# A third raw query block in the last two heads, with part of its subtractions on VectorE, and three late gate and up tiles moved into the rounds

## The chip, the cores and the metric

The kernel runs on one core of one Trainium2 chip. A core has a matrix engine (TensorE, PE in the profile), VectorE (DVE), ScalarE (ACT), GpSimd (POOL) and SyncE (SP), which here only issues transfers. Each engine works through its own instructions in order, and they wait for each other by semaphores. Matrix results go to PSUM, everything else lies in SBUF. The metric is the time of one execution in microseconds of device time; less is better.

## The reference

The result is a mix of an attention block and a gated MLP, with a gate per row:

```python
x = A_x                                             # 1 x 2048 x 448
g = _sigmoid((x * gate_w).sum(-1, keepdims=True))
# attention, 16 heads of 28 columns
scores = jnp.einsum("bhqd,bhkd->bhqk", q, k) * (Dh ** -0.5)
p = _softmax(scores, axis=-1)
a = einsum("bhqk,bhkd->bhqd", p, v) ... @ wo
# MLP, 1792 hidden columns
gate = gate * (gate > 0)
b = (gate * up) @ W_down
return g * a + (1 - g) * b
```

All is float32. The kernel splits most matmul operands into a high and a low part and sums several products (`TERMS`, 11 products for one contraction).

## The kernel before

**Stages.** First come the projections to Q, K and V. Then come 32 *rounds*, two for each of the 16 heads: round v works on *visit* v, which is head v // 2 with one half of its 2048 keys. Last comes a tail with the down projection of the MLP, the output projection and the result.

**A visit.** The 2048 queries of a head are four blocks j = 0 to 3 of 512 queries; the visit's 1024 keys are eight chunks of 128. A *score pair* (`score`, letter s) is two matmuls of 128 keys x 512 queries into one PSUM tile of two banks. There are three such tiles in turn (`ps_w`). A visit has 16 pairs, four for each block. Four chunks of one block are a *quad* in SBUF, 128 x 2048; ten slots hold quads.

**Two ways to the softmax.** The scores need a maximum per query subtracted before the exponential.

- A block that is not raw gets its maximum beforehand: TensorE computes scores the other way round (`smax`, letter m, two matmuls into a PSUM tile) and VectorE reduces them (L228, 128 x 1024). The maxima are written as two extra rows into Q, and the score matmul subtracts them by itself. ScalarE then takes the exponential straight from PSUM (L334).
- A *raw* block needs no maxima from TensorE. ScalarE copies its negated scores to SBUF (L336). VectorE takes a running minimum over the pairs (`block_min`, letter b, L280; three instructions for four pairs, and all but the first pair are read from PSUM, so the tile is held until then). `all_max` (letter A, L295 to L303) reduces over the partitions and spreads the result over a tile `rm`. GpSimd subtracts `rm` from each of the block's two quads (`take_max`, letter g, L309, 128 x 2048), and ScalarE takes the exponential in SBUF (L320; letter e half a quad, E a whole one). When the second visit of a head changes the maximum, the first visit's sums are rescaled (`rescale`, letters c and f).

`RAW` names the raw blocks of each visit: blocks 3 and 2 everywhere, except in the very first visit. So the maxima of a head are 16 pairs: two blocks x four groups of 128 queries x two halves.

**P and Q** (`pv`) multiply the exponentials with V, 64 TensorE instructions for the two parts of a round. P needs the first quad of every block, Q the second.

**x** is one matmul of the projections that are computed between the attention's: until round 3 part of Q and K (L641), then gate and up of the MLP (L633). 22 x's are one tile of 128 hidden columns x 512 rows: 11 for gate, then 11 for up. Its result h is stored to memory (`spill_h`). There are 56 tiles; `done` of them are computed in the rounds, the rest (`gate_up`) in the tail.

**The order** is written out by hand, one letter for each step: `ROUNDS` holds a string for each round. Each letter issues its instructions to all the engines that take part, and every engine keeps the order in which they were issued; nothing reorders them. Four score pairs of the next visit are always issued in the round ahead (`AHEAD`). Other letters: n ends a head's maxima, N normalises the head before, w splits a weight tile, D prepares the first weights of the down projection.

**The tail.** A list `todo` is worked off: 12 matmuls for each of 56 hidden tiles (`down`), whose operand h is fetched and split by ScalarE and VectorE (L136, L142), the remaining `gate_up` tiles between, and the output projection (`wout`) when the last head has been normalised, stored, fetched again and split.

Of the kernel before, what the change touches and what calls it, by code (L numbers as in the profile page):

```python
# [8 lines left out]
F32 = mybir.dt.float32  # L9
# [3 lines left out]
OP = mybir.AluOpType  # L13
AX = mybir.AxisListType
# [4 lines left out]
P = 128  # L19
# [7 lines left out]
NF = F // P  # L27
NB = 4
# [9 lines left out]

RAW = [(3,), (3, 2), (3, 2), (3, 2)]

# [6 lines left out]
NP = 10  # L47

R11 = "ssbnsxxxxsxbxNxbxxggsxxxxsxxxsxsxxssxxAmxsxxemsxmxexxmxsmxxemmgexsbxxxsbcxxxsbxAxmgeePefeQ"

R12 = "gsmsxxxxssebxxbbxxxsxxxxmxAexxssxgsxxsxxsxxmxxsxxemsmexgxexmxxxmsxmxexsbxsgebsebAPQ"

# [21 lines left out]

R29 = "sxxsxsxxxbxgxsxxbsxExsxxxxxxxxxbxssxsxAxxxsxgNxxsxsxxxssxxxxgxsxxxExxxbxgxxbxExsexxcxexfxPbAQn"

R30 = "sgsxxsbxxsxxxxxbxxgxEbxxxxxsxxxxxsssxxxxxsxxsxAsxxxxexgxxxxsxsExxxsexxxbgxxxxsexbxxsexDDbxPQA"

R31 = "sxsxxsxxxbxxxxxsbbxxxxxxxgsxxxxsxxssxxxxAsxxsxxgxgxgExxxDxxxxNxxxExxEsexcexxsxxfxxxDxPQ"

# [3 lines left out]
    R12, R11, R12, R11, R12, R11, R12, R11,  # L84
    R12, R11, R12, R11, R12, R29, R30, R31,
]
# [13 lines left out]
def gated_mix_kernel(ctx, tc, x, wq, wo, wgu, wd, out):  # L100
# [101 lines left out]
    def raw(v):  # L202

        return RAW[v] if v < len(RAW) else RAW[len(RAW) - 2 + v % 2]

# [85 lines left out]
    def all_max():  # L291
        v, j, quads = todo_all.pop(0)
        to = ((0, 11) if j == 2 else (9, 10))[v % 2]
        a, b = (1 - v % 2, 9) if j == 2 else (1, 9 + v % 2)
        nc.vector.tensor_reduce(MN[:, 1:3], R2.pop((v, j)).rearrange("p a (b r) -> p a b r", r=32), axis=AX.X, op=OP.min,  # L295
                                apply_transpose=True)
        move(MN[:64, 3:5], MN[64:, 1:3])
        move(MN[:32, 5:9], MN[32:64, 1:5])
# [4 lines left out]
        nc.vector.transpose(RM[v, j], MN[:, to].unsqueeze(2).to_broadcast([P, 16, 32]))  # L303
        todo_sub.extend((v, j, q) for q in quads)

    def take_max():
        v, j, q = todo_sub.pop(0)
        m = RM[v, j].unsqueeze(1).to_broadcast([P, 4, TB])
        nc.gpsimd.tensor_tensor(QUAD[q], QUAD[q], m, op=OP.subtract)  # L309
        todo_exp.append(q)  # L310
# [355 lines left out]
    def rescale(v, part):  # L666

        h = v // 2
        if v % 2 == 0:
            return  # L670
        rows = slice(64, P)
        if part == 0:
            RS[h] = fe.tile([P, TB], F32, name=f"rs_{h}", tag="rb", bufs=1)
            for r, a, b in ((slice(64, 96), 11, 0), (slice(96, P), 10, 9)):
                nc.gpsimd.tensor_tensor(MN[r, 1], MN[r, a], MN[r, b], op=OP.subtract)
            nc.vector.transpose(RS[h][rows], MN[rows, 1].unsqueeze(2).to_broadcast([64, 16, 32]))
        else:
# [97 lines left out]
    for v, order in enumerate(ROUNDS):  # L775
# [4 lines left out]
        for o in order:  # L780
# [159 lines left out]
    def down(i):  # L940
# [6 lines left out]
        if f == NF - 1:  # L947
# [9 lines left out]
            (fetch_w, 6), (fetch_w, 7), (lambda: wor.append(load_wo()),), (fetch_h, 6), (gate_up, done), (spread, H - 1),  # L957
            (split_wd, 4), (fetch_w, 8), (split_wd, 5), (fetch_w, 9), (fetch_h, 7), (gate_up, done + 1)]
    for i in range(NB * NF):
# [63 lines left out]
```

## Time and profile before

| | us |
|---|---|
| median of 3 runs | 1185.54 (1185.16 to 1185.97) |
| the profiled execution | 1184.21 |
| its span from the first to the last instruction | 1182.4 |
| TensorE matmuls busy | 1175.0 |
| VectorE busy | 894.1 |
| ScalarE busy | 877.2 |
| GpSimd busy | 743.3 |
| rounds 25 to 31 (794.1 to 985.8) | 191.7 |
| the tail (985.8 to 1182.4) | 196.6 |

A row of the profile names the line, the engine, the operation, the tiles as out<-in, the shapes and the count; behind the bar stand the busy time, the mean duration of one in ns, and the idle time of the engine ahead of these instructions with what ended it. In a timeline row the start and the duration stand first. PEld is TensorE's loading of weights, which runs beside its matmuls. Matmul durations in the rows overlap, so the cost of one is read from the distance of many.

### The profile page before, as it was taken

Reading aid. Unit: us, or ns where it says so; the run is one execution under the profiler, and the core shown is the slowest. Engines: PE = TensorE matmul, PEld = TensorE weight load, DVE = VectorE, ACT = ScalarE, POOL = GpSimd, SP = SyncE. Lnnn points to the kernel's source line nnn. Section 1 sums busy time; section 2 is a strip of 40 time slices with the busy share of each in tenths; the row PEclk is TensorE's granted clock in tenths of the full one; section 3 lists DMA queues with packets and bytes.
Section 4 is the critical chain, followed back from the end, with each engine's and each line's share of the span. In section 5 each row is a group of like instructions: output and inputs, shape, how many; then the busy total and the mean of one; then the engine's idle time right before and its main releaser. Section 6 shows DMA issues by size and latency. Waiting matters only on the chain.

```text
span 1182.4 us, 17006 instructions
## 1 busy us (share of the span) xinstructions
PE 1175.0 (99%) x6183; PEld 821.2 (69%) x6183; DVE 894.1 (76%) x1173; ACT 877.2 (74%) x1054; POOL 743.3 (63%) x325
## 2 busy tenths in 40 slices
PE   9999999999999999999999999999999999999998
PEld 6886666666666666666666666666666667899997
DVE  6577898888988898989898888889898553444242
ACT  5237889899999988888888887888888885322121
POOL 5323667888988886777777766767676784422020
PEclk9999999999999999999999999999999999999999
DMA  9994565636373754343446535153444437644342
GB/s 322 280 394 142 186 210 172 185 124 196 117 216 108 205 167 139 119 128 92 119 136 212 140 102 153 49 152 109 139 154 156 129 100 231 209 152 118 115 134 75
DMA packets 70667, 188.85 MB, mean 160 GB/s; under 512 B 13958, under 2 KB 20558, under 8 KB 65678
## 3 DMA queue, kind: packets, MB, share of 16 engines
q1 hardware_dynamic: 65624, 167.31, 45.9%
q0 software_dynamic: 4480, 19.99, 4.5%
q8 instruction: 48, 0.79, 0.3%
q10 hardware_dynamic: 480, 0.47, 0.1%
q14 instruction: 35, 0.29, 0.1%
HBM read 126.96 MB, written 60.96 MB: 159 GB/s over the span
## 4 chain that ended last, share of the span: by engine, by line
PE 96%; DVE 1%; DMA 1%; ACT 1%; issue 0%; SPq 0%; DVEq 0%; ACTq 0%
PE gu L633 24%; PE s L330 20%; PE po L692 19%; PE acc L927 12%; PE sm L224 10%; PE v L469 3%; PE wo L886 3%; PE qk L641 3%; PE qk L454 2%; DVE r L280 1%; DMA wr<-wq 0%; DMA X<-x_d 0%; ACT P L336 0%; ACT V L336 0%; SPq L414 0%
## 5 line engine op out<-in xcount | busy, mean ns | idle before, releaser
L309 POOL TENSOR_TENSOR P<-P,rm 128x2048 f32<-128x2048 f32 x102 | 470.8, 4635 | 107.9 <-DVE rm L303 84.1
L633 PE MATMUL gu<-X,wg 128*128 128x512 f32 x1232 | 358.9, 395 | 0.1
L228 DVE TENSOR_REDUCE mx<-sm 128x1 f32<-128x1024 f32 x256 | 302.9, 1217 | 43.0 <-PE sm L224 42.1
L330 PE MATMUL s<-Q,K 128*128 128x512 f32 x1024 | 315.9, 403 | 1.7 <-DVE mx L228 0.9
L633 PEld LDWEIGHTS gu<-X,wg 128*128 128x128 f32 x1232 | 231.2, 188 | 57.6 <-issue 1.7
L330 PEld LDWEIGHTS s<-Q,K 128*128 128x128 f32 x1024 | 180.7, 188 | 82.4 <-DVE r L280 10.4
L336 ACT ACTIVATE P<-s 128x1024 f32<-128x1024 f32 x204 | 202.2, 1028 | 42.0 <-PE s L330 39.6
L692 PE MATMUL po<-P,V 128*32 128x512 f32 x1640 | 227.4, 594 | 0.0
L334 ACT ACTIVATE P<-s 128x1024 f32<-128x1024 f32 x206 | 201.4, 1040 | 14.1 <-PE s L330 13.1
L320 ACT ACTIVATE P<-P 128x1024 f32<-128x1024 f32 (+1 forms) x182 | 208.5, 1171 | 0.5 <-POOL P L309 0.2
L224 PE MATMUL sm<-K,Q 128*128 128x512 f32 x520 | 163.2, 400 | 0.1
L280 DVE SCALAR_TENSOR_TENSOR r<-s,r 128x1024 f32<-128x1024 f32 x124 | 151.6, 1223 | 13.6 <-ACT P L336 6.0
L692 PEld LDWEIGHTS po<-P,V 128*32 128x32 f32 x1640 | 62.6, 110 | 113.3 <-issue 109.6
L692 PE MATMUL po<-V 128*32 128x512 f32 x408 | 136.2, 594 | 0.0
L309 POOL TENSOR_TENSOR V<-V,rm 128x2048 f32<-128x2048 f32 x24 | 111.2, 4635 | 26.1 <-DVE rm L303 22.6
L224 PEld LDWEIGHTS sm<-K,Q 128*128 128x128 f32 x520 | 91.9, 188 | 34.1 <-ACT P L334 4.6
L136 ACT ACTIVATE hh<-hr 128x512 fp32r<-128x512 f32 x52 | 32.8, 632 | 109.5 <-PE acc L927 109.4
L142 DVE TENSOR_TENSOR hh<-hr,hh 128x512 fp32r<-128x512 f32 x52 | 47.3, 915 | 72.6 <-ACT hh L136 72.5
L927 PE MATMUL acc<-WD,hh 128*128 128x448 f32 x480 | 99.5, 366 | 0.0
L927 PEld LDWEIGHTS acc<-WD,hh 128*128 128x128 f32 x480 | 90.2, 188 | 7.3 <-DVE hh L142 0.2
L280 DVE SCALAR_TENSOR_TENSOR r<-s,P 128x1024 f32<-128x1024 f32 x50 | 61.1, 1223 | 33.3 <-ACT P L336 33.0
L295 DVE TRANSPOSE_TENSOR_REDUCE mn<-r 128x32 f32<-128x1024 f32 x63 | 78.1, 1239 | 1.3
(93 smaller groups left out, 1135.5 us busy)
## 6 DMA issues: line engine op xcount, KB each, us to landing
wg<-ws_d SPq DMA_DIRECT2D x42, 896.0 KB
K<-qk_d SPq DMA_DIRECT2D x32, 448.0 KB
X<-x_d SPq DMA_DIRECT2D x56, 256.0 KB
h_d<-h SPq DMA_DIRECT2D x56, 256.0 KB
Q<-qk_d SPq DMA_DIRECT2D x62, 224.0 KB
hr<-h_d SPq DMA_DIRECT2D x52, 256.0 KB
ws_d<-wg SPq DMA_DIRECT2D x14, 896.0 KB
x_d<-X POOLq DMA_DIRECT2D x8, 1024.0 KB, 15.2
```

The lines of the kernel that those rows point to most:

```text
L224: nc.tensor.matmul(ps[:, c, :], Q[h][:, u * P:(u + 1) * P], K[h % 3][:, k0:k0 + TB], start=True, stop=True)
L228: nc.vector.tensor_reduce(to, ps, axis=AX.XY, op=OP.max)
L280: nc.vector.scalar_tensor_tensor(r, ps, -1.0, before, op0=OP.mult, op1=OP.min)
L295: nc.vector.tensor_reduce(MN[:, 1:3], R2.pop((v, j)).rearrange("p a (b r) -> p a b r", r=32), axis=AX.X, op=OP.min, apply_transpose=True)
L309: nc.gpsimd.tensor_tensor(QUAD[q], QUAD[q], m, op=OP.subtract)
L320: nc.scalar.activation(q, q, AF.Exp, scale=-SCALE)
L330: nc.tensor.matmul(ps[:, c], K[h % 3][:, k * P:(k + 1) * P], Q[h][:, j * TB:(j + 1) * TB], start=True, stop=True)
L334: nc.scalar.activation(dst, ps, AF.Exp, scale=SCALE)
L336: nc.scalar.activation(dst, ps, AF.Copy, scale=-1.0)
L633: nc.tensor.matmul(ps, WS[i][:, s, a], xf(i // NF, b), start=(n == 0), stop=(n == NT - 1))
L692: nc.tensor.matmul(po[32 * j:32 * j + 32], V[:, h // 4 % 2, k, h % 4], AT.pop((v, k, j)), start=(k == k0), stop=(k == k0 + NK // 2 - 1))
L927: nc.tensor.matmul(ACC[i // NF][t][:, :D], HH[i][:, a, t * P:(t + 1) * P], wd_high_low(f, b), start=(f == 0 and n == 0), stop=(f == NF - 1 ...
```

## The change

- In visits 28 to 31, the last two heads, block 1 is raw too (`RAW`). Their maxima are then for block 0 alone, 8 pairs a head instead of 16. The third raw block gets its own columns of the small tile `MN` in `all_max`, and `rescale` covers all four blocks' rows there.
- A new letter G is a subtraction of `rm` that is issued to VectorE instead of GpSimd: one in round 25, two in 26, one in 28, two in 29, one in 30, two in 31.
- Three more gate and up tiles, 66 x's, are in the rounds (`done` is 55 instead of 52), so the tail has one left.
- The strings of rounds 25 to 31 are new. Rounds 0 to 24 are as before; their strings only stand in another order in the file.

```diff
-RAW = [(3,), (3, 2), (3, 2), (3, 2)]
+RAW = [(3,)] + [(3, 2)] * 27 + [(3, 2, 1)] * 4
...
-R30 = "sgsxxsbxxsxxxxxbxxgxEbxxxxxsxxxxxsssxxxxxsxxsxAsxxxxexgxxxxsxsExxxsexxxbgxxxxsexbxxsexDDbxPQA"
+R28 = "sxxssbbgsbxxxExxsgxxxxsxsxxxsAxEbxxgxxxxxbxxxbxxgAxsxsxxxxxxGsxssxxxxxmxxmExsEgxxxxbxxxxxxExsxesbbexAPQxxx"
...
+R30 = "DxxDxsxsxxxxxgbxsxgbssxxbxsExxxAxsxxxxbsbxxbxxExxxgxxxAxxxxgsxGsxxsxxsxsExExsxxExxgexessxxxxxxbxbxxxxxxxPQxxbA"
...
-    R12, R11, R12, R11, R12, R29, R30, R31,
+    R12, R25, R26, R27, R28, R29, R30, R31,
...
-        to = ((0, 11) if j == 2 else (9, 10))[v % 2]
-        a, b = (1 - v % 2, 9) if j == 2 else (1, 9 + v % 2)
+        c = 12 if j == 1 else 0
+        to = ((12, 21), (0, 11), (9, 10))[j - 1][v % 2]
+        a, b = (c + 1 - v % 2, c + 9) if j < 3 else (1, 9 + v % 2)
...
-    def take_max():
+    def take_max(engine):
         v, j, q = todo_sub.pop(0)
         m = RM[v, j].unsqueeze(1).to_broadcast([P, 4, TB])
-        nc.gpsimd.tensor_tensor(QUAD[q], QUAD[q], m, op=OP.subtract)
+        engine.tensor_tensor(QUAD[q], QUAD[q], m, op=OP.subtract)
         todo_exp.append(q)
...
-    MN = att.tile([P, 12, 16], F32, name="mn")
+    MN = att.tile([P, 22, 16], F32, name="mn")
...
-        rows = slice(64, P)
+        more = 1 in raw(v)
+        rows = slice(0 if more else 64, P)
...
-            for r, a, b in ((slice(64, 96), 11, 0), (slice(96, P), 10, 9)):
+            for r, a, b in ((slice(0, 32), 21, 21), (slice(32, 64), 21, 12), (slice(64, 96), 11, 0), (slice(96, P), 10, 9))[0 if more else 2:]:
...
-            elif o == "g":
-                take_max()
+            elif o in "gG":
+                take_max(nc.gpsimd if o == "g" else nc.vector)
```

In the rows of the order below, `r2_28_1` is the running minimum of visit 28, block 1; `rm_28_1` the spread maximum; `P_28_1_0` (or `V_103`, two slots that lie in V) a quad of this block; `sm` a tile of the maxima's scores; `h_44` the product of a gate and up tile. Line numbers of the change are 8 to 10 higher.

VectorE in round 28, behind the spreading of block 2's maximum. Before:

```order
L303 STREAM_TRANSPOSE rm_28_2_8082<-mn_891 128x512
L707 RECIPROCAL rq_13_8090<-ls_13_8017 128x16
L228 TENSOR_REDUCE mx_15_7864<-sm_254_8128 128x1
L652 TENSOR_TENSOR h_43_8142<-gu_43_1_8088,rl_43_8086 128x512
L228 TENSOR_REDUCE mx_15_7864<-sm_255_8149 128x1
```

Now:

```order
L312 STREAM_TRANSPOSE rm_28_2_8058<-mn_891 128x512
L288 SCALAR_TENSOR_TENSOR r2_28_1_8062<-s_28_2_1_8032,P_28_1_0_8014 128x1024
L288 SCALAR_TENSOR_TENSOR r2_28_1_8062<-s_28_4_1_8038,r2_28_1_8062 128x1024
L661 TENSOR_TENSOR h_43_8076<-gu_43_1_8045,rl_43_8043 128x512
L288 SCALAR_TENSOR_TENSOR r2_28_1_8062<-s_28_6_1_8048,r2_28_1_8062 128x1024
L304 TENSOR_REDUCE mn_891<-r2_28_1_8062 128x32
...
L312 STREAM_TRANSPOSE rm_28_1_8093<-mn_891 128x512
L318 TENSOR_TENSOR P_28_1_0_8014<-P_28_1_0_8014,rm_28_1_8093 128x2048
L236 TENSOR_REDUCE mx_15_7811<-sm_242_8135 128x1
L236 TENSOR_REDUCE mx_15_7811<-sm_243_8141 128x1
```

A second block's minima and reduction and one subtraction (L318) now stand where there were only maxima, and the two maxima that are left stand behind the subtraction.

GpSimd in the same round. Before:

```order
L309 TENSOR_TENSOR P_28_3_0_7910<-P_28_3_0_7910,rm_28_3_7969 128x2048
L309 TENSOR_TENSOR V_103<-V_103,rm_28_3_7969 128x2048
L309 TENSOR_TENSOR V_103<-V_103,rm_28_2_8082 128x2048
L309 TENSOR_TENSOR P_28_2_1_8042<-P_28_2_1_8042,rm_28_2_8082 128x2048
```

Now:

```order
L318 TENSOR_TENSOR P_28_3_0_7867<-P_28_3_0_7867,rm_28_3_7938 128x2048
L318 TENSOR_TENSOR V_103<-V_103,rm_28_3_7938 128x2048
L318 TENSOR_TENSOR V_103<-V_103,rm_28_2_8058 128x2048
L318 TENSOR_TENSOR P_28_2_1_7993<-P_28_2_1_7993,rm_28_2_8058 128x2048
L318 TENSOR_TENSOR P_28_1_1_8037<-P_28_1_1_8037,rm_28_1_8093 128x2048
```

GpSimd has a fifth subtraction, for the second quad of block 1; the first quad's is VectorE's.

VectorE in round 29, behind the last spreading of a maximum of this visit (block 2 before, block 1 now). Before:

```order
L303 STREAM_TRANSPOSE rm_29_2_8353<-mn_891 128x512
L652 TENSOR_TENSOR h_45_8385<-gu_45_1_8339,rl_45_8328 128x512
L280 SCALAR_TENSOR_TENSOR r2_30_3_8421<-s_30_2_3_8396,P_30_3_0_8391 128x1024
L280 SCALAR_TENSOR_TENSOR r2_30_3_8421<-s_30_4_3_8407,r2_30_3_8421 128x1024
L676 STREAM_TRANSPOSE rs_14_8438<-mn_891 64x512
```

Now:

```order
L312 STREAM_TRANSPOSE rm_29_1_8395<-mn_891 128x512
L318 TENSOR_TENSOR V_103<-V_103,rm_29_1_8395 128x2048
L686 STREAM_TRANSPOSE rs_14_8413<-mn_891 128x512
L661 TENSOR_TENSOR h_47_8432<-gu_47_1_8397,rl_47_8381 128x512
L318 TENSOR_TENSOR P_29_1_3_8330<-P_29_1_3_8330,rm_29_1_8395 128x2048
L288 SCALAR_TENSOR_TENSOR r2_30_3_8446<-s_30_2_3_8419,P_30_3_0_8405 128x1024
```

Both subtractions of block 1 are VectorE's here, and the transpose of the rescaling, which waits for small subtractions on GpSimd, stands between them.

More of the change, by code (lines that the diff above doesn't have):

```diff
@@ L47 @@
 NP = 10
-R11 = "ssbnsxxxxsxbxNxbxxggsxxxxsxxxsxsxxssxxAmxsxxemsxmxexxmxsmxxemmgexsbxxxsbcxxxsbxAxmgeePefeQ"
-R12 = "gsmsxxxxssebxxbbxxxsxxxxmxAexxssxgsxxsxxsxxmxxsxxemsmexgxexmxxxmsxmxexsbxsgebsebAPQ"
 R0 = "bsxxsbxxxxbsxxssAxxxxxxsxxsxxxmsxxgsxxxxmxsxxsxbgxxxxxxxxbEsxxemxbxxxmxeAPQ"
@@ L202, in raw @@
     def raw(v):
-        return RAW[v] if v < len(RAW) else RAW[len(RAW) - 2 + v % 2]
+        return RAW[v]
     def rows_of(h):
@@ L957, in gated_mix_kernel @@
             (fetch_w, 6), (fetch_w, 7), (lambda: wor.append(load_wo()),), (fetch_h, 6), (gate_up, done), (spread, H - 1),
-            (split_wd, 4), (fetch_w, 8), (split_wd, 5), (fetch_w, 9), (fetch_h, 7), (gate_up, done + 1)]
+            (split_wd, 4), (fetch_w, 8), (split_wd, 5), (fetch_w, 9), (fetch_h, 7)]
+    if done + 1 < NB * NF:
+        todo.append((gate_up, done + 1))
     for i in range(NB * NF):
```

18 lines of the change are left out of this document (12 added, 6 removed).

## The prediction

> **What bounds the kernel now.** I read the page's shares and its chain of waits first, then the stretches that the change touches, then the spacing of TensorE's instructions.
>
> ```profile
> PE 1175.0 (99%) x6183; PEld 821.2 (69%) x6183; DVE 894.1 (76%) x1173; ACT 877.2 (74%) x1054; POOL 743.3 (63%) x325
> PE 96%; DVE 1%; DMA 1%; ACT 1%; issue 0%; SPq 0%; DVEq 0%; ACTq 0%
> core 0: us, PE busy (x) PEld busy (x) DVE busy (x) ACT busy (x) POOL busy (x), PEclk, DMA share, GB/s
> 794.10:985.80 191.70, 191.53 (x1051) 123.44 (x1051) 139.88 (x194) 168.26 (x185) 142.76 (x46) 1.00 0.41 128
> 985.80:1182.40 196.60, 192.77 (x940) 175.82 (x936) 79.11 (x101) 51.34 (x81) 38.86 (x31) 1.00 0.48 149
> 478.69 0.93 PE sm L224 x4
> 925.84 7.00 PE po L692 x64
> 1018.51 5.14 PE gu L633 x22
> ```
>
> TensorE ends nearly every wait (96% of the chain), at a granted clock of 1.00. A 512-column matmul comes every 5.14/22 = 0.2335 us, and a maxima matmul costs the same (0.93/4). The 64 instructions of P and Q take 7.00 us a round. The row 794.1 to 985.8 is rounds 25 to 31, the row behind it the tail. In those rounds stand 319 x's, 108 score pairs and 32 maxima pairs: 599 matmuls x 0.2335 = 139.9, with seven P and Q 188.9 us. Measured are 191.7, so only 2.8 us are transposes and waits: the stretch runs at TensorE's own pace.
>
> **What is removed and moved.** 16 maxima pairs go, 32 matmuls x 0.2335 = **7.5 us** off TensorE. The 66 matmuls of the moved tiles (15.4 us) leave the tail and enter the rounds: nothing in the sum, as long as both places stay full. So the rounds now hold 633 matmuls, 147.8 + 49.0 = 196.8 us. Beside it a small gain: at the last change of X, the matmul behind it now has a transpose, a maxima pair and five score pairs (3 us) between, where before it waited:
>
> ```profile
> L633 PEld LDWEIGHTS gu<-X,wg 128*128 128x128 f32 x22 | 4.1, 188 | 1.7 <-DMA X<-x_d 0.8
> ```
>
> I take 0.8 us for it. With all else as before, 1184.2 (the profiled execution's own time) becomes 1175.9, or 1177.2 on the scale of the median, which lies 1.3 above that execution.
>
> **What is added on ScalarE and VectorE.** The third raw block costs each of visits 28 to 31 two quads of exponentials, three running minima (b), a reduction (A) and two subtractions.
>
> ```profile
> 849.30:877.80 28.50, 28.36 (x158) 18.03 (x154) 25.15 (x35) 25.09 (x29) 21.12 (x8) 1.00 0.38 125
> 877.80:905.10 27.30, 27.30 (x150) 17.08 (x150) 24.06 (x32) 23.45 (x26) 17.46 (x4) 1.00 0.52 170
> 844.65 2.54 DVE L280 SCALAR_TENSOR_TENSOR r<-s,r 128x1024 f32<-128x1024 f32 x2
> 847.23 1.25 DVE L295 TRANSPOSE_TENSOR_REDUCE mn<-r 128x32 f32<-128x1024 f32 x1
> 849.85 0.71 DVE L303 STREAM_TRANSPOSE rm<-mn 128x512 f32<-128x512 f32 x1
> 891.55 5.75 DVE L228 TENSOR_REDUCE mx<-sm 128x1 f32<-128x1024 f32 x5
> 910.33 0.68 DVE L652 TENSOR_TENSOR h<-gu,rl 128x512 f32<-128x512 f32 x1
> 914.17 5.63 ACT L334 ACTIVATE P<-s 128x1024 f32<-128x1024 f32 x6
> 922.61 1.91 ACT L320 ACTIVATE P<-P 128x2048 f32<-128x2048 f32 x1
> L142 DVE TENSOR_TENSOR X<-xr,X x8: 692/956/1225, 5.3 to 23.4; 128x512 fp32r<-128x512 f32 x4, 128x1024 fp32r<-128x1024 f32 x4
> ```
>
> From start to start a b takes (847.23 - 844.65)/2 = 1.29, an A 849.85 + 0.71 - 847.23 = 3.33, a maxima reduction 1.15, h 0.7. A subtraction on VectorE has two inputs in SBUF; the nearest row takes 0.69 for 512 columns and 1.225 for 1024, so 2048 give 1.225 + 2 x 0.53 = 2.29 (two of the larger would be 2.45; I take 2.3). VectorE in round 28: nine b 11.6, three A 10.0, two maxima 2.3, one G 2.3, three h 2.1, one addition 0.7 = **29.0 us**, where TensorE has 96 matmuls and 7.0, 29.4 us. Round 29: 11.6 + 10.0 + two G 4.6 + h 2.1 + 1.0 of small ones = 29.3 of 29.9. Round 30: 26.7 of 29.7; round 31: 22.5 of 30.1. Before, VectorE was busy 25.15 of 28.5 in round 27 and 24.06 of 27.3 in 28: 88%. Now it stands at 98% for two rounds, before any wait. ScalarE in round 28: 16 pairs at 5.63/6 = 0.94, five whole exps 9.6, two halves 2.1, 2.2 of relus and a copy = 28.9 at most of 29.4, and neighbours overlap; nothing in the sum, but no cover either. I take 0.9 us for this density beyond the 2.8 that the stretch lost before (bounds 0 and 4 us: 0 if the old slack was never needed, 4 if 6% of slack is needed in both rounds).
>
> **What the subtractions on VectorE meet.** GpSimd's subtractions take 4.6 us each. The trace has two places that tell what a VectorE instruction with two SBUF inputs does beside GpSimd:
>
> ```profile
> 906.18 9.23 POOL L309 TENSOR_TENSOR P<-P,rm 128x2048 f32<-128x2048 f32 x2 [7.70 <-DVE rm L303]
> L142 DVE TENSOR_TENSOR hh<-hr,hh x52: 678/693/2889, 1002.9 to 1172.0; 128x512 fp32r<-128x512 f32 x52
> 1124.08 0.69 DVE L142 TENSOR_TENSOR hh<-hr,hh 128x512 fp32r<-128x512 f32 x1 [1.74 <-ACT hh L136]
> 1127.94 6.55 DVE L142 TENSOR_TENSOR hh<-hr,hh 128x512 fp32r<-128x512 f32 x4 [3.17 <-ACT hh L136]
> 1127.47 5.22 POOL L145 TENSOR_TENSOR on<-or,on 128x1024 fp32r<-128x1024 f32 x2 [32.74 <-ACT on L136]
> L145 POOL TENSOR_TENSOR on<-or,on x6: 2399/2409/2791, 1053.7 to 1129.9; 128x1024 fp32r<-128x1024 f32 x6
> ```
>
> Alone, hh takes 0.69. Four of them beside two GpSimd instructions take 6.55 instead of 2.8, the longest 2.889: it stood 2.2 us, nearly a whole GpSimd instruction of 2.4. No hh took 4.8, so VectorE got through between the two; GpSimd's second was longer by 0.38. The two do not run at once. The Trainium skill's page "SBUF — State Buffer", section "Who interferes with whom", says the same more sharply: the shared ports are an exclusive lock, and the second to issue "**fully blocks**" until the first is done; it leaves open who comes next when both wait. The trace agrees on the block (2.889 against 0.69 us) and settles the turn for hh. Were the next turn GpSimd's, G would wait 4.6 us more in rounds 28 and 30 each, 9.2 us on top of the sum below; by the row it is nothing.
>
> So where does GpSimd stand when a G comes? In rounds 28 to 30 the g's of block 2 are released by its A; behind this A VectorE runs three b, an h and the next A, 3.9 + 0.7 + 3.3 = 7.9 us, while GpSimd has two g's, 9.2 us. The G meets the second g and waits at least 1.3 us. In round 28 the count from the end of block 3's A is four g's, 18.5 us, against 0.7 + 1.4 + 7.7 + 6.7 = 16.5: G waits 2.0. Behind it on VectorE stand two maxima reductions that hold two of TensorE's three score tiles, and the exp for P. In round 29 the four small subtractions of the rescaling, for rows like
>
> ```profile
> 925.93 0.49 POOL L675 TENSOR_TENSOR mn<-mn 32x16 f32<-32x16 f32 x2
> 893.85 4.64 POOL L309 TENSOR_TENSOR P<-P,rm 128x2048 f32<-128x2048 f32 x1
> 901.27 1.10 ACT L320 ACTIVATE P<-P 128x1024 f32<-128x1024 f32 x1
> 898.12 7.00 PE po L692 x64
> ```
>
> (four now: 1.0 us), stand behind the G, and VectorE's transpose behind them: 1.3 + 0.4 more. In round 30 the copies for the down weights put GpSimd later: 1.3 to 2.6, I take 1.9. In round 31 both G's come behind two g's, and the normalising multiplication (1.3 us) goes between them: 1.0 to 2.4, I take 1.7. In rounds 25 and 26 GpSimd is idle or nearly so when the G's come: 0. Does VectorE's delay reach TensorE? The last rows say so: the last g of round 28 ended at 898.49, its second exp at 902.37, in Q's first microsecond (P and Q began at 898.12). There was hardly any slack. So the collisions cost 2.4 (2.0 and the part of P's exp) + 1.7 + 1.9 + 1.7 = **7.7 us**, bounds 0 (the delays fall into waits of TensorE's own) and 9 x 4.6 = 41 us (each G behind a whole g); the rows lie near the low end, since GpSimd is late by 1 to 2 us only.
>
> **The tail.** It loses 15.4 us of matmuls that lay ahead of the first output projection.
>
> ```profile
> 1005.98 1.29 POOL L718 TENSOR_TENSOR ox<-ox,rb 128x512 f32<-128x512 f32 x1 [11.30 <-DMA rb<-l_d]
> 1012.04 0.43 SPq L870 DMA_DIRECT2D or<-o_d  x1
> 1025.18 1.05 ACT L136 ACTIVATE on<-or 128x1024 fp32r<-128x1024 f32 x1
> 1030.95 2.23 PE wo L886 x11
> ```
>
> The projection began 45.1 us into the tail (985.8); now it is due at 29.7. Its chain on SP's queue: spread comes behind gate_up's store of h, one tile (5.1 us) earlier now, so the fetch of o issues at 21 us instead of 26.2. The fetch landed at some time before 1025.18, within 13 us. If it needs all of these, with 2 us for the splitting, the projection is late by some 6 us. At the tail's mean of 149 GB/s the 1 MB takes 7 us, which with the splitting ends at 30, and the weight tiles that loaded the queues are gone. I take 0, bounds 0 and 6.
>
> **Sum.** 1184.2 - 7.5 - 0.8 + 0.9 + 7.7 + 0 = 1184.5; on the median's scale 1185.8 us.
>
> **The rivals.** (a) Forecast: the collisions eat the saving, 1185.8, own range 1183 to 1188.5; chance 0.40. (b) The collisions are absorbed: VectorE waits for TensorE's score tiles often enough that G comes when GpSimd is done, or P and Q find their exps ready. Then 1185.8 - 7.7 = 1178.1, with 0.4 of leftovers 1178.5. For it speaks that VectorE idled 12% before; against it that this idling is gone in rounds 28 and 29. 0.28. (c) Slower: VectorE becomes the bound of rounds 28 and 29, because its idle time (3.3 us a round before, waits for data in order) doesn't vanish when its work grows. Round 28: 29.0 + 2.0 + 3.3 = 34.3 against 29.4, +4.9; round 29: 29.3 + 1.7 + 3.3 = 34.3 against 29.9, +4.4; round 30: 26.7 + 1.3 + 3.3 = 31.3, +1.6; round 31 +1.7: 12.6 in place of 8.6, so 1189.8. It decides once more than half of the old idle time stays. For it speaks the order: b's release score tiles, and A's stand before them. Against it, a VectorE that is behind finds its data ready. 0.27. (d) The tail's cover is missing: +3 to 6, 1190. 0.05.
>
> **How the numbers follow.** The likeliest is (a): 1185.8. The range reaches (b) and (c): 1177.5 to 1191.5. A measurement of this kernel tells about 0.2% (2.4 us) from no change: faster is below 1183.2, slower above 1187.9. Of (a)'s 0.40, 0.05 falls below, 0.27 within and 0.08 above; (b) gives 0.27 faster and 0.01 same; (c) and (d) give 0.05 same and 0.27 slower. Faster 0.32, same 0.33, slower 0.35.
>
> **What would show it.** The maxima row has 488 matmuls, gate and up in the tail 22. (a): the subtractions on VectorE in rounds 28 to 31 last 3.5 us or more, in round 26 2.3; rounds 25 to 31 take 205 to 209 us; waits of TensorE's queue for VectorE appear there. (b): the same stretch takes under 201 us, whatever the G's last. (c): VectorE is busy over 95% in rounds 28 and 29 and these take 34 us each. (d): TensorE idles before its first projection. I am wrong at the root if G's of 2.3 us run beside g's under way, or if TensorE's loss lies in rounds 25 to 27.

## The result: 11 us slower than before, outside the predicted range

| | before | after |
|---|---|---|
| median | 1185.76 (1185.16 to 1187.34) | 1196.61 (1195.43 to 1198.48) |
| ratio, 95% interval | | 1.0091 (1.0076 to 1.0106) |
| profiled span | 1182.4 | 1195.1 |
| rounds 0 to 24 end at | 794.1 | 796.7 |
| rounds 25 to 31 | 191.7 | 213.0 |
| tail | 196.6 | 185.4 |

The forecast was 1185.8 us with a range of 1177.5 to 1191.5. "Slower" had a chance of 0.35; the range ends 5 us short of the result.

Busy time by engine and the shares of the chain of waits, on the page of the changed kernel:

```profile
PE 1174.7 (98%) x6151; PEld 814.1 (68%) x6151; DVE 933.8 (78%) x1206; ACT 891.1 (75%) x1055; POOL 751.6 (63%) x328
PE 82%; DVE 6%; DMA 5%; POOL 2%; ACT 2%; issue 2%; SPq 1%; DVEq 0%; ACTq 0%; POOLq 0%
```

TensorE executes 32 matmuls fewer, as the change says, and yet its share of the chain of work that ended last falls from 96% to 82%. The chain leaves TensorE where something else ended last, so the share does not give TensorE's loss; it says that VectorE, transfers, GpSimd and ScalarE now end last in places. The next view is the same stretch of rounds 27 to 31 that was read before, one row a round (end of Q to end of Q; columns as in the prediction):

```profile
848.90:878.40 29.50, 28.94 (x155) 17.21 (x151) 25.89 (x37) 25.03 (x28) 21.34 (x8) 1.00 0.38 120
878.40:910.40 32.00, 30.56 (x163) 19.06 (x160) 28.20 (x39) 27.56 (x26) 26.29 (x6) 1.00 0.54 172
910.40:943.50 33.10, 31.52 (x167) 20.56 (x168) 28.21 (x36) 29.87 (x31) 23.03 (x10) 1.00 0.37 125
943.50:975.20 31.70, 31.13 (x160) 19.44 (x160) 23.50 (x33) 27.43 (x26) 26.79 (x7) 1.00 0.36 121
975.20:1009.60 34.40, 31.99 (x169) 20.93 (x166) 29.25 (x35) 26.13 (x27) 28.11 (x12) 1.00 0.36 118
```

By the letters of the orders, 0.2335 us for each 512-column matmul, 7.0 for P and Q and the transposes, these rounds need 26.9, 29.4, 30.2, 29.65 and 30.1 us. Each takes more: 2.6, 2.6, 2.9, 2.05 and 4.3. With rounds 25 and 26 (27.4 and 24.8, where 26.45 and 25.0 are needed) TensorE loses 15.3 us in this stretch. VectorE, which I feared as the bound, is busy 28.2 of 32.0 and 28.2 of 33.1 us, 88% and 85%.

Now the nine subtractions on VectorE (start, duration; x2 is two in one row) and what GpSimd does beside some of them, from the two engines' timelines:

```profile
811.67 2.47 DVE L318 TENSOR_TENSOR P<-P,rm 128x2048 f32<-128x2048 f32 x1
837.35 2.28 DVE L318 TENSOR_TENSOR P<-P,rm 128x2048 f32<-128x2048 f32 x1
840.88 2.28 DVE L318 TENSOR_TENSOR P<-P,rm 128x2048 f32<-128x2048 f32 x1
896.10 3.96 DVE L318 TENSOR_TENSOR P<-P,rm 128x2048 f32<-128x2048 f32 x1
929.24 3.85 DVE L318 TENSOR_TENSOR V<-V,rm 128x2048 f32<-128x2048 f32 x1
935.22 2.27 DVE L318 TENSOR_TENSOR P<-P,rm 128x2048 f32<-128x2048 f32 x1
961.97 3.91 DVE L318 TENSOR_TENSOR P<-P,rm 128x2048 f32<-128x2048 f32 x1
995.17 9.24 DVE L318 TENSOR_TENSOR P<-P,rm 128x2048 f32<-128x2048 f32 x2
```

```profile
812.08 2.42 POOL L685 TENSOR_TENSOR mn<-mn 32x16 f32<-32x16 f32 x2
893.26 11.25 POOL L318 TENSOR_TENSOR P<-P,rm 128x2048 f32<-128x2048 f32 x2
963.67 6.68 POOL L318 TENSOR_TENSOR V<-V,rm 128x2048 f32<-128x2048 f32 x1
989.76 9.21 POOL L318 TENSOR_TENSOR P<-P,rm 128x2048 f32<-128x2048 f32 x2
998.94 3.32 POOL L728 TENSOR_TENSOR ox<-ox,rb 128x512 f32<-128x512 f32 x1
```

Alone it takes 2.28 us: in round 26 and at 935.22 GpSimd has no subtraction under way. Beside a GpSimd subtraction it takes 3.85 to 3.96 in rounds 28 to 30, and in rounds 28 and 30 GpSimd's next one is stretched from 4.63 to 6.65 (11.25 for two, 6.68 for one). In round 25 it meets two small subtractions of the rescaling, which take 2.42 in place of 0.49. In round 31 two take 9.24, and GpSimd's normalising multiplication 3.32 in place of 1.29. The Trainium skill's page "SBUF — State Buffer", section "Who interferes with whom", says that a VectorE instruction with two SBUF inputs contends with a GpSimd instruction that reads SBUF, and that the ports they share are an exclusive lock. These rows agree, and show that each in turn is stopped for what is left of the other's instruction.

How it reaches TensorE is in the chain of waits of round 28 (start, us, what):

```profile
896.10 3.96 DVE P L318
900.07 2.28 DVE mx L236 x2
902.39 0.73 PE s L339 x2
903.36 7.00 PE po L702 x64
```

The maxima reductions stand behind the subtraction on VectorE and hold score tiles; the score behind them waits, then P.

TensorE's own waits over rounds 25 to 31 (for what, us in total, times, longest) name the two things that P needs, the exponentials and a free PSUM tile, and the score tiles (for the kernel before this list is empty). The last two rows are of its weight loads, which wait for the same things ahead of the matmuls:

```profile
PE po L702 <- ACT P L329: 2.5, 2, 2.4
PE po L702 <- DVE h L661: 1.6, 1, 1.6
PE s L339 <- DVE r L288: 1.0, 3, 0.4
PE s L339 <- DVE mx L236: 0.9, 2, 0.7
PEld po L702 <- ACT P L329: 6.5, 6, 3.3
PEld s L339 <- DVE r L288: 4.6, 11, 0.7
```

The matmuls' own waits sum to 6.4 us with two small ones more; the rest of the 15.3 is not put down to single causes by these lists.

The tail: chain of waits, TensorE's timeline, and ScalarE's split of the output weights in the kernel before (first row) and now:

```profile
1014.77 7.12 DMA wor<-wo_d
1021.92 1.34 ACT WO L144
1031.87 7.33 DMA or<-o_d
1039.22 1.07 ACT on L144
```

```profile
1027.22 14.46 PE L937 MATMUL acc<-WD,hh 128*128 128x448 f32 x70 [2.15 <-DVE hh L150]
1045.24 0.68 PE L896 MATMUL wo<-WO,on 128*128 128x448 f32 x2 [1.68 <-DVE on L150]
```

```profile
999.34 1.78 ACT L136 ACTIVATE WO<-wor 128x1344 fp32r<-128x1344 f32 x2
1021.92 1.79 ACT L144 ACTIVATE WO<-wor 128x1344 fp32r<-128x1344 f32 x2 [3.88 <-DMA wor<-wo_d]
```

The output weights' split stands ahead of the splits of h on ScalarE and VectorE and waits 3.88 us for its fetch, issued 5 us into the tail. Before, when it did not wait, one more tile of 5.1 us stood ahead of it on TensorE, and three more ahead of the first output projection. Now TensorE waits 2.15 us for h, and 1.68 more for o.

### The profile page after: what moved, and what is told of

The parts are those of the page before. It is cut to its first block, busy times and chain, and to the rows that moved or that the text cites. A ratio compares the mean times of both kernels' runs of the same rounds, so it can differ in the third digit from the quotient of the medians.

```text
span 1195.1 us, 17014 instructions
## 1 busy us (share of the span) xinstructions
PE 1174.7 (98%) x6151; PEld 814.1 (68%) x6151; DVE 933.8 (78%) x1206; ACT 891.1 (75%) x1055; POOL 751.6 (63%) x328
## 4 chain that ended last, share of the span: by engine, by line
PE 82%; DVE 6%; DMA 5%; POOL 2%; ACT 2%; issue 2%; SPq 1%; DVEq 0%; ACTq 0%; POOLq 0%
PE gu L642 19%; PE po L702 19%; PE s L339 18%; PE acc L937 9%; PE sm L232 9%; PE wo L896 3%; PE qk L650 3%; PE v L478 2%; DVE r L288 2%; POOL P L318 1%; DMA Q<-qk_d 1%; DMA X<-x_d 1%; DVE P L318 1%; DMA or<-o_d 1%; DMA wor<-wo_d 1%
## 5 line engine op out<-in xcount | busy, mean ns | idle before, releaser
L318 POOL TENSOR_TENSOR P<-P,rm 128x2048 f32<-128x2048 f32 x100 | 463.4, 4651 | 105.8 <-DVE rm L312 78.3
L236 DVE TENSOR_REDUCE mx<-sm 128x1 f32<-128x1024 f32 x240 | 284.4, 1217 | 44.1 <-PE sm L232 43.2
L329 ACT ACTIVATE P<-P 128x1024 f32<-128x1024 f32 (+1 forms) x184 | 218.5, 1215 | 8.7 <-DVE P L318 6.7
L288 DVE SCALAR_TENSOR_TENSOR r<-s,r 128x1024 f32<-128x1024 f32 x132 | 161.4, 1223 | 19.8 <-ACT P L345 10.7
L232 PE MATMUL sm<-K,Q 128*128 128x512 f32 x488 | 153.5, 400 | 1.3 <-DMA Q<-qk_d 1.0
L702 PE MATMUL po<-V 128*32 128x512 f32 x408 | 143.8, 594 | 0.0
L318 POOL TENSOR_TENSOR V<-V,rm 128x2048 f32<-128x2048 f32 x25 | 117.8, 4715 | 35.8 <-DVE rm L312 35.6
L232 PEld LDWEIGHTS sm<-K,Q 128*128 128x128 f32 x488 | 86.2, 188 | 33.8 <-ACT P L343 5.2
L288 DVE SCALAR_TENSOR_TENSOR r<-s,P 128x1024 f32<-128x1024 f32 x53 | 64.6, 1219 | 25.8 <-ACT P L345 25.5
L304 DVE TRANSPOSE_TENSOR_REDUCE mn<-r 128x32 f32<-128x1024 f32 x67 | 83.0, 1239 | 1.3
```

What stands on the lines that cost most here:

```text
L232: nc.tensor.matmul(ps[:, c, :], Q[h][:, u * P:(u + 1) * P], K[h % 3][:, k0:k0 + TB], start=True, stop=True)
L236: nc.vector.tensor_reduce(to, ps, axis=AX.XY, op=OP.max)
L288: nc.vector.scalar_tensor_tensor(r, ps, -1.0, before, op0=OP.mult, op1=OP.min)
L304: nc.vector.tensor_reduce(MN[:, c + 1:c + 3], R2.pop((v, j)).rearrange("p a (b r) -> p a b r", r=32), axis=AX.X, op=OP.min, apply_transpos ...
L318: engine.tensor_tensor(QUAD[q], QUAD[q], m, op=OP.subtract)
L329: nc.scalar.activation(q, q, AF.Exp, scale=-SCALE)
```

## Experiments

Theory T: the loss is the forecast's collisions, larger than forecast, and the uncovered fetches in the tail. Rivals: VectorE is simply too full; the moved tiles themselves cost; the rounds' new orders cost. "Rounds" are rounds 25 to 31 of the profile. Medians and ratios are against runs of the kernel before made beside them (1184.9 to 1185.6).

| run | median | ratio (interval) | rounds | tail |
|---|---|---|---|---|
| port_free | 1187.34 | 1.0019 (1.0009 to 1.0029) | 204.0 | 185.7 |
| tail_order | 1193.67 | 1.0076 (1.0063 to 1.0089) | 212.8 | 184.0 |
| both | 1184.20 | 0.9991 (0.9982 to 1.0) | 204.1 | 185.0 |
| before_tail | 1185.99 | 1.0003 (0.9994 to 1.0012) | 192.1 | 196.5 |
| port_late | 1187.63 | 1.0031 (1.002 to 1.0042) | 204.9 | 185.9 |
| no_sub | 1184.13 | 0.9998 (0.9989 to 1.0006) | 204.4 | 185.5 |
| all_pool | 1211.36 | 1.0214 (1.02 to 1.0228) | 228.5 | 187.5 |
| tiles_only | 1193.76 | 1.0073 (1.006 to 1.0086) | 210.9 | 187.7 |
| raw_only | 1214.33 | 1.0251 (1.0237 to 1.0266) | 223.1 | 196.5 |
| one_head | 1200.98 | 1.0131 (1.0117 to 1.0145) | 213.8 | 191.5 |
| one_head_same | 1201.94 | 1.0144 (1.0129 to 1.016) | 210.7 | 191.4 |
| both_r27 | 1187.76 | 1.002 (1.0011 to 1.0029) | 207.0 | 181.8 |
| r27_spread | 1185.63 | 1.0006 (0.9997 to 1.0015) | 207.3 | 181.9 |
| gap | 1196.32 | 1.0093 (1.0079 to 1.0107) | 203.3 | 196.7 |

### The collisions

```diff
 def take_max(engine):
 ...
-    engine.tensor_tensor(QUAD[q], QUAD[q], m, op=OP.subtract)
+    if engine is nc.vector:
+        engine.tensor_reduce(QUAD[q][:, 0, 0:1], QUAD[q], axis=AX.XY, op=OP.min)
+    else:
+        engine.tensor_tensor(QUAD[q], QUAD[q], m, op=OP.subtract)
```

> The changed kernel, but each of VectorE's nine subtractions is replaced by a reduction of the same 128x2048 quad to one column of it: about the same 2.3 us on VectorE at the same place in its order, with one input in SBUF instead of two. These nine quads are left without their maximum subtracted, so that part of the softmax is left out. Theory 1 (the two engines shut each other out over their SBUF inputs): the nine instructions last 2.3 us each, no GpSimd subtraction is longer than 4.7, rounds 25 to 31 fall from 213 us to 203 to 206, the total from 1196.6 to 1187 to 1190. Rival (VectorE is simply full in rounds 28 to 30, port or not): the rounds fall by 2 us at most, 1195.

Measured: 1187.34, rounds 204.0: **9.3 us** of the 11 come back (9.0 in the rounds). VectorE has the same quads to read and the same time to spend (2.24 to 2.28 us each), but with one SBUF input it does not stop GpSimd. It also writes one column instead of 2048; the minima, which have one SBUF input too and write 1024 columns, take at most 1.227 us throughout the changed kernel, so the writing alone does not make the two collide. GpSimd's subtractions of the P quads (100 of its 125) now all take 4.6, minimum, median and maximum in ns:

```profile
L321 POOL TENSOR_TENSOR P<-P,rm x100: 4599/4634/4667, 103.4 to 986.6; 128x2048 f32<-128x2048 f32 x100
```

In the changed kernel the maximum of that row is 6648. The rival (VectorE is full) falls. By round, from 25 to 31, the changed kernel takes 0.7, 0, 0.1, 1.5, 1.5, 1.4 and 3.7 us more than this run.

Where do they cost? port_late has that edit only for `v > 27`; the three in rounds 25 and 26 subtract.

> The changed kernel, with VectorE's subtraction replaced by the read-only reduction only in rounds 28 to 31 (six quads go into the exponential without their maximum subtracted); the three of rounds 25 and 26, which run while GpSimd is idle, stay. Theory (a subtraction costs where it meets GpSimd's, not by itself): the whole gain of the first such run stays, 1186.7 to 1188 us, rounds 25 to 31 at 204. Rival (each subtraction on VectorE costs, wherever it is, a ninth of the 9.3 us): 1190.4 us.

Measured: 1187.63, 0.3 us above the run with all nine replaced (1.4 by the two ratios), rounds 204.9 in place of 204.0. So the six late ones cost nearly the whole. The two of round 26, beside an idle GpSimd, cost nothing that shows (24.9 us, 24.8 without them). The one of round 25 does cost: the round takes 27.4 us as in the changed kernel, 26.7 without it, and the rescaling's two small subtractions take 2.43 us in place of 0.49.

And VectorE's load? no_sub is the run called both (below) with nothing at all in the nine places (`if engine is nc.gpsimd:` ahead of the subtraction).

> The run with both edits, and VectorE's nine reductions of 2.28 us left out altogether (nine quads go into the exponential without their maximum subtracted), so that VectorE has 20.5 us less work in rounds 25 to 31 and nothing of the port. What is left of VectorE's density in the run with both edits is its difference to this one. My term for the density was 0.9 us with bounds 0 and 4. Theory (the density costs little, the rest of the 6.4 us that rounds 25 to 31 still lose there is order): 1182.5 to 1184.2 us, rounds 202.5 to 204. Rival (VectorE's added work is what remains): 1179 to 1181, rounds 199 to 200.5.

Measured: 1184.13 beside 1184.20, rounds 204.4 and 204.1. 20.5 us less work on VectorE change nothing, though its busy share falls from 85% and 84% in rounds 28 and 29 to 79% and 70%. The load of the nine costs **0**, and the 4 us that the rounds lose beyond my count do not come from it. The third block's minima and reductions are still in this run; no run takes them out.

all_pool turns every G into g.

> All nine subtractions go to GpSimd, none to VectorE, the same places in the order. Theory (a subtraction on either of the two engines stops the other, so VectorE's part costs GpSimd what it saves it): GpSimd then needs 4.6 us for each in place of the 2.3 that VectorE has the port, so the last exponentials of rounds 28, 29, 30 come about 2.3 us later, those of round 31 and the three in rounds 25 and 26 too; VectorE gets 20 us back, which releases score tiles earlier. Sum 1196.6 + 9 x 2.3 less what VectorE's early release gives (about half): 1200 to 1215 us, rounds 217 to 231. Rival (the density of VectorE is the loss): VectorE falls from over 90% to about 80% in rounds 28 to 31 and the time falls below 1193.

Measured: 1211.36, in the range of the theory. Even blocked, VectorE's nine are worth 14.8 us: the pair is one resource, and VectorE holds it 2.28 us for what takes GpSimd 4.63. Some 7 of the 14.8 are TensorE's work at half clock after the longer waits (13.65 us of it in this profile), which the last section explains.

### The tail

```diff
-            ..., (fetch_w, 7), (lambda: wor.append(load_wo()),), (fetch_h, 6), (gate_up, done), (spread, H - 1),
+            ..., (fetch_w, 7), (fetch_h, 6), (gate_up, done), (spread, H - 1), (lambda: wor.append(load_wo()),),
...
-    before(1, (normalise, H - 1), (lambda: split_wo(wor[0]),))
+    before(1, (normalise, H - 1))
+    before(6, (lambda: split_wo(wor[0]),))
```

> The changed kernel, but in the tail the output projection's weights are fetched behind the spreading of the last row sums instead of ahead of it, and split before hidden tile 6 instead of tile 1. Nothing is left out. Theory 1 (the tail lost 4.2 of its 15.4 us because that fetch of 7 us stands ahead of the splits on ScalarE and VectorE, and delays the last head's chain): the tail falls from 185.4 us to 181 to 183, total 1192 to 1194. Rival (the tail waits for data that come late anyway, from the last round): no change, 1196.6.

Measured: 1193.67, 2.9 us less by the medians (1192.55 to 1195.80, where the changed kernel has 1195.43 to 1198.48); tail 184.0, a little above the 181 to 183 expected.

before_tail is the same edit in the kernel before.

> The kernel before with only the tail's reordering (output weights fetched behind the spread of the row sums, split ahead of the sixth down product). Theory (the tail of the kernel before had three more tiles of 5.1 us that covered these fetches, the change took the cover away): nothing to gain here, 1184.6 to 1186.2 us, tail 196 to 197. Rival (the tail always lost this): tail 193.5 to 194.5, 1182.5 us.

Measured: 1185.99, nothing, with the tail at 196.5. So the old order is harmless where the three tiles stand, and the change made it cost.

both has the edits of port_free and tail_order.

> Both edits at once: VectorE's nine subtractions are read-only reductions of the quad (so nine quads go into the exponential without their maximum subtracted), and the tail fetches and splits the output weights late. If the collisions and the order of the tail are two separate losses, the savings of the two single runs add: 1196.6 - 9.3 - 2.9 = 1184.4 us, rounds 25 to 31 at 204, the tail at 183 to 184. Rival: they are one loss seen twice (the late end of round 31 makes the tail's fetches late), then little comes on top of the larger one: 1187 us, tail 185.5.

Measured: 1184.20; the sum was 1184.4. The two losses are separate and make up the whole difference: the tail's edit gives 3.1 us here too. Without them the change is within 0.1% of the kernel before. (The tail of 185.0 is that of a profiled execution 2.0 us above this median; see the last section.)

### One part of the change alone

tiles_only: the kernel before, with 22 x's more, spread evenly, in each of rounds 29, 30 and 31 (and three tiles fewer in the tail). raw_only: the changed kernel, with 16 or 17 x's taken from each of rounds 28 to 31 evenly, so that no tile is moved.

> The kernel before with one part of the change alone: three more gate and up tiles in rounds 29 to 31, 22 x's spread evenly over each of the old strings; no third raw block, no subtraction on VectorE. Theory 1 (the rounds take the tiles at TensorE's pace, but the tail misses its cover): rounds 25 to 31 take 206 to 207.5 us instead of 191.7, the tail 185 to 186 instead of 196.6, total 1189 to 1191. Rival (the move is free): rounds 207, tail 181, total 1185.8 as before.

Measured: 1193.76, 3 us above. Rounds 29 and 30 take 32.6 us each, where their letters need 32.45: nothing is lost. Round 31 takes 34.4 and needs 30.6; its end, from the chain of waits:

```profile
984.53 0.72 DVE rm L303
985.40 4.65 POOL P L309
990.07 3.72 ACT P L320 x2
996.25 5.29 PE po L692 x29
```

With x's spread evenly the scores, the maximum and the subtractions all come later. The relu whose tile P needs stands on ScalarE behind those exponentials; P waits 2.0 us for it, and the clock is then 0.50 for 3.4 us. So moving the tiles costs by itself, in round 31 and in the tail (187.7, where 181.2 were due); 1.7 us of each is the low clock.

> The changed kernel without the moved tiles: 66 x's taken out evenly from the strings of rounds 28 to 31, so that the tail has its four gate and up tiles again; the third raw block, VectorE's subtractions and the order of all else as changed. Theory 1 (rounds 28 to 31 are paced by VectorE's chain and by the port, the x's fill TensorE's gaps): the rounds lose less than 8 us of the 15.4 (205 or more), the tail takes 196.6, total 1199 to 1203. Rival (TensorE still sets the pace, stalls are a fixed extra): rounds 198, tail 196.6, total 1192 to 1193.

Measured: 1214.33, 11 us above the highest that I had allowed. With less work for TensorE the rounds are longer: round 29 39.6 us where the changed kernel takes 33.1. TensorE's timeline, and the windows around that wait (the third number from the right is the granted clock):

```profile
940.43 1.06 PE L702 MATMUL po<-P,V 128*32 128x512 f32 x1 [6.26 <-DVE h L661]
```

```profile
935.00:940.00 5.00, 0.00 (x0) 0.00 (x0) 4.24 (x4) 5.00 (x4) 0.61 (x3) 0.62 0.29 119
940.00:946.00 6.00, 5.57 (x28) 1.36 (x32) 5.65 (x10) 3.81 (x6) 2.98 (x3) 0.50 0.13 46
946.00:949.00 3.00, 3.00 (x26) 0.81 (x22) 0.11 (x1) 0.00 (x0) 3.00 (x2) 0.93 0.00 0
```

P waits for the product h, which frees its PSUM tile and stands on VectorE behind the subtractions. After this wait the granted clock is 0.50 for some 6 us: P's 32 instructions take 6.6 us in place of 3.5. Is it the wait that does it? gap is the kernel before with one long wait added:

```diff
-R31 = "...AsxxsxxgxgxgExxx..."
+R31 = "...AsxxsxxgxgxgzzExxx..."
+            elif o == "z":
+                q = todo_exp[-1]
+                again = not again
+                nc.gpsimd.tensor_tensor(QUAD[q], QUAD[q], RM[q[:2]]..., op=OP.add if again else OP.subtract)
```

> The kernel before, with two more GpSimd instructions of 4.6 us behind the last subtraction of round 31 (they add the maximum to the quad again and subtract it once more), so that TensorE waits once for some 8 us ahead of the last half of its last output product. Theory (after a wait of several us TensorE's clock is granted at half for 5 to 6 us, as in rounds 29 and 31 of the run with the raw blocks alone): the wait costs itself and 2.5 to 3 us more: about 1185.6 + 8.4 + 2.8 = 1196.8 us, with a granted clock of 0.50 in the 4 us behind the wait. Rival (the low clock there had another cause): clock 1.00, 1194 us.

Measured: 1196.32. The wait and the windows behind it:

```profile
992.15 2.78 PE L692 MATMUL po<-P,V 128*32 128x512 f32 x10 [7.44 <-ACT P L320]
997.89 7.30 PE L633 MATMUL gu<-X,wg 128*128 128x512 f32 x30
```

```profile
985.00:990.00 5.00, 0.00 (x0) 0.00 (x0) 0.00 (x0) 0.00 (x0) 4.92 (x2) 0.98 0.00 0
990.00:994.00 4.00, 1.85 (x12) 0.54 (x16) 0.06 (x1) 2.91 (x3) 3.77 (x5) 0.50 0.00 0
994.00:996.00 2.00, 2.00 (x16) 0.46 (x12) 1.34 (x2) 1.20 (x2) 0.56 (x1) 0.50 0.52 115
996.00:998.00 2.00, 2.00 (x13) 0.41 (x5) 0.00 (x0) 0.00 (x0) 1.85 (x2) 0.85 0.98 158
```

TensorE waited from 984.7 to 992.15. The 28 matmuls left of Q need 28 x 0.109 = 3.1 us and took 5.7 (992.15 to 997.89): **2.7 us** on top of the wait. In the profile of the changed kernel, which waits 2.4 us at most at a time, the clock stays whole (1.00 in each row above); what decides is in the last section.

### One head instead of two

one_head has `RAW = [(3,)] + [(3, 2)] * 29 + [(3, 2, 1)] * 2`, the kernel before's rounds up to 29, and the changed kernel's 30 and 31 with three and five x's fewer.

> The third raw block only in visits 30 and 31 (the last head): rounds 25 to 29 are the kernel before's, rounds 30 and 31 the changed kernel's, shortened by three and five gate-up matmuls, so that one tile and not three moves from the tail into the rounds. 16 maxima matmuls fall (3.7 us), 22 matmuls come in (5.1). Theory (the losses are those of the rounds with a third raw block, by the place of the subtractions): rounds 30 and 31 lose their 2.1 and 4.3 us as in the changed kernel, others nothing; rounds 25 to 31 at 191.7 - 3.7 + 5.1 + 5.5 = 198.6, the tail 191.5 + 1 to 2; 1185.4 to 1188. Rival (the losses grow through the rounds: lateness is handed on from round 27 to 31): round 31 in time again, 195 for the rounds, 1182 to 1183.

Measured: 1200.98, 13 us above. Round 30 takes 42.8 us: P waits 6.88 us for a relu that stands on ScalarE behind exponentials and copies of scores, six instructions in the time of the wait; then P and Q take 9.88 at the low clock.

one_head_same keeps rounds 30 and 31 to the letter, and takes eight x's from round 29.

> The third raw block only in visits 30 and 31, as in the run with one head, but rounds 30 and 31 are the changed kernel's to the letter, and round 29 (the kernel before's, less eight gate-up matmuls) ends at the same place within a tile as the changed kernel's round 29. In the run with one head a tile's end stood elsewhere: there P of round 30 waited 6.9 us for the relu of a tile that stood on ScalarE behind six exponentials. Theory (the 15 us lost there come from where the tiles end among the other work): rounds 30 and 31 take the 31.7 and 34.4 us of the changed kernel, one tile is moved, and the time falls from 1201 to 1190 to 1193 us. Rival (two heads are needed to get the raw blocks going, one head alone starts round 30 too late): round 30 above 38 us again, 1198 to 1203.

Measured: 1201.94; the theory falls. Round 30 does come down, to 34.2, and round 31 is at the changed kernel's 34.4; but now round 29, with nothing new in it save eight x's fewer, takes 32.9 where it needs 25.5: P waits 3.8 us for a relu, and P and Q take 8.8 us. In these two runs the place of a tile's end decides where the wait lies, not whether there is one.

### Round 27

With both losses gone (both) the rounds still lose 6.4 us, 2.5 of them in round 27, where VectorE subtracts nothing. Two orders of that round were tried on the kernel called both.

```diff
-    R12, R25, R26, R27, R28, R29, R30, R31,
+    R12, R25, R26, R11, R28, R29, R30, R31,
```

> The run with both edits, and round 27 in the kernel before's order (the two of its maxima that the changed kernel puts into round 28 come in it, the rest of the work is the same). Round 27 of the changed kernel takes 29.5 us where its matmuls and transposes take 26.9, though VectorE subtracts nothing there: the reduction behind the second block stands ahead of four maxima reductions on VectorE. Theory (the new order of round 27 costs 2 us by itself): rounds 27 and 28 together 57.5 to 58.5 in place of 59.9, 1182 to 1183 us. Rival (round 27 waits for what round 26 hands on): 59.5 to 60.5, 1184 us.

Measured: 1187.76; rounds 27 and 28 take 62.8 us in place of 59.9.

```diff
-R27 = "xsxxxxxsxxxgxbxxsbxsxxsxxxsbxxnsmgsssxxxssAxmxEmmsxm...
+R27 = "xsxxxsxxgxbxxsbxsxxsxxsbxnsxmgsxsxsxxsxsAxxmxEmxmsxm...
```

> The run with both edits, with the 26 gate-up matmuls of the first part of round 27 spread between its score pairs (the rest of the order unchanged). In that run TensorE loses 2.2 us there in small waits, most of them for ScalarE, which has seven exponentials of 0.94 us in a row while the scores come 0.5 us apart. Theory (bunched scores are the loss of round 27): round 27 at 27.5 to 28 in place of 29.4, 1182 to 1183 us. Rival (the loss is VectorE's order, the reduction ahead of the maxima): 29.4 again, 1184.2 us.

Measured: 1185.63; round 27 takes 32.6. Now TensorE waits 1.6 us at once for a maxima reduction of VectorE, and the clock falls behind this wait (last section). Both theories fall, and what round 27 loses is left open: the order that stands is the best of the three.

## Why the prediction was wrong

The profiled executions give the account (forecast 1184.5 on its scale, measured 1195.1 + 1.8 = 1196.9): **+5.6 in the rounds, +4.2 in the tail, +2.6 ahead of round 25**.

- **Maxima, 7.5 us: right as a count.** 32 matmuls fewer, 0.2335 us each; no run shows this saving by itself.
- **Subtraction of 2.3 us and the block: right.** 2.28 alone, 3.85 to 3.96 beside GpSimd in rounds 28 to 30, a wait of 1.6 to 1.7 where 2.0, 1.3 and 1.3 were forecast. That VectorE gets through between two GpSimd instructions holds too (the two of 11.25 us are 2.0 longer than 9.25, as VectorE's instruction went between).
- **Collisions, 7.7 us: mechanism right, size low.** port_free puts them at 9.3 (9.0 in the rounds). Rounds 28 to 30 cost less than forecast (1.5, 1.5 and 1.4 in place of 2.4, 1.7 and 1.9), round 25 cost 0.7 where I had 0, and the term that was mis-sized is round 31's: I had 1.7 for both, and the round loses 3.7; the two take 9.24 - 4.56 = 4.7 us longer. I had let them come when GpSimd was nearly done. But GpSimd's two subtractions ahead begin only at 989.76, so the first waits most of one of 4.6 us, the second for the normalising multiplication.
- **Density, 0.9 us, and rival (c): not borne out.** no_sub shows 0 for the load of the nine. VectorE was 85 to 88% busy in rounds 28 and 29, not over 95%. Rival (c) named a time nearer to the result (1189.8) for a reason that does not hold.
- **The other waits, taken as the 2.8 us of before: too low by some 4.** With the collisions gone the rounds take 204.0, where 199.7 follow from my terms; 2.5 of it are round 27's. I had taken it that new orders fill TensorE as well as the old, and the runs of this study show how little that is given: of the orders changed by hand only round 26 of the changed kernel and rounds 29 and 30 of tiles_only lost nothing. What the 4 us come from is otherwise open. The 0.8 us for X did come: TensorE's waits of this stretch no longer name X.
- **"The moved tiles: nothing in the sum, as long as both places stay full", and "the tail: 0, bounds 0 and 6": this failed.** The tail lost 4.2 us, inside those bounds but not in the sum; and tiles_only shows the move costing 3.8 us in round 31 as well. I had weighed the fetch of o alone and had not followed the output weights, whose split stands in front of h on two engines. Rival (d) had this mechanism with a chance of 0.05, and as another case beside (a), where it comes on top of (a). That is why the range did not hold: (a) with 9.3, (d) with 4 and some 4 of new waits add up.
- **Ahead of round 25, 2.6 us: no effect of the change.** Those orders are the same, and over all sixteen profiles their end varies from 794.1 to 796.7, and the changed kernel's profile has the latest.
- The sign of "wrong at the root" did not come: some 12 of the 15.3 us lie in rounds 28 to 31, and no subtraction of 2.3 us ran beside a GpSimd subtraction.

No run is clearly faster than the kernel before. The one that comes nearest, both, leaves nine subtractions out and is still within 0.1% of the kernel before: with its 9.3 us of collisions the change cannot win by the tail's reordering alone (1193.67).

## What to carry to other kernels

Two engines that cannot read SBUF at the same time are one resource: work moved from one to the other is worth at most the difference of their durations (4.63 less 2.28 us here), and only where the first is idle is it free. When work leaves a place, look at each instruction that waits for a transfer behind it and at what stands in order behind that instruction, all of them and not only the last operand. Effects in several places add; rivals with one cause each are not a range.

## What was not expected of the hardware

**A wait can cost twice.** After a TensorE wait of 7.44 us (gap) the granted clock was 0.50 from 989.7 to 996.6, from 5.0 us after its last matmul to 4.4 us after its next; after 6.26 us (raw_only) it was 0.50 for some 6 us of work; after 6.88 (one_head) P and Q took 9.88 in place of 7.0. After the waits of 2.2 to 2.4 us in the changed kernel's profile it stayed 1.00 (its other executions have mean clocks of 0.997 to 0.999). The Trainium skill's page "TensorE: Matmul & The Clock Gate", section "HAM oscillation — how this bites in real kernels", has the rule that idle gaps over about 3.4 us bring the clock down to half. For the waits of 3.6 us and more these runs agree, with a price for one gap of 2.7 us. For shorter ones they do not, and the measurement decides: the clock fell after a single wait of 1.58 us (r27_spread, first two rows), and not after one of 2.41 (one_head_same, last two):

```profile
860.91:864.32 3.41, 1.70 (x7) 0.78 (x5) 3.31 (x7) 2.03 (x2) 2.08 (x1) 1.00 0.82 253
864.32:867.73 3.41, 3.37 (x8) 2.70 (x9) 2.34 (x2) 1.65 (x2) 3.41 (x2) 0.50 0.31 121
```

```profile
996.41:999.82 3.41, 1.72 (x16) 0.55 (x20) 3.41 (x2) 2.83 (x3) 3.41 (x2) 1.00 0.17 38
999.82:1003.23 3.41, 3.36 (x36) 0.94 (x32) 1.70 (x3) 3.38 (x4) 1.12 (x4) 1.00 0.77 263
```

The windows are cut at steps of 3.41 us for a reason. Apart from the last 3 us of the span, nine of the sixteen profiles have a low clock. There it is low for 3.4, 6.8 or 10.2 us, and the low pieces of one run begin a whole number of 3.41 us apart (raw_only: 902.0, 936.1, 1007.9). Cut in such steps, from 60 us to 12 us ahead of the end, all nine show the same: after a step in which TensorE was busy 1.58 us or less the next one has 0.50, after 1.72 or more it has 1.00 (1.67 and 1.70 went one way each), and the low clock ends behind a step that TensorE fills nearly whole (3.25 or more). So it is not the length of one wait that counts, but whether about half of one such step is empty, and where the steps begin differs from run to run.

This is part of why the runs with fewer matmuls in the rounds were slower: raw_only's TensorE works 14.3 us at half clock, some 7 of the 25.5 us that its rounds lose more than the changed kernel's. x's do not only fill the rounds, they keep the clock up.

**The tail has two paces.** The last block of 120 down matmuls, in the timelines of the run called both, and of both_r27, which has the same tail:

```profile
1155.62 24.96 PE L940 MATMUL acc<-WD,hh 128*128 128x448 f32 x120
```

```profile
1154.87 24.48 PE L940 MATMUL acc<-WD,hh 128*128 128x448 f32 x120
```

2% apart, at a clock of 1.00 in both, and held over the whole tail from about 1031 us: 3 us in all. both and no_sub have the longer one throughout, tail_order and tiles_only in the last blocks, all others the shorter. At the shorter pace the reordered tail takes 181.8 (both_r27), 4 us less than the 185.4 to 185.9 without it: nearly the whole of the tail's loss, where tail_order's median shows 2.9. What sets the pace is open. The profiled executions of both and no_sub are 2.0 and 2.5 us above their medians, so it may differ between executions of one kernel; no two traces of one kernel are there to show it.
